# Scaling and splitting v on GpSimd, and one product in place of two for the remainder rows

## The chip, the cores and the metric

The kernel runs on one core of one Trainium2 chip. The metric is the device time of one execution in microseconds (us). The core has five engines that run side by side, each with a queue of its own that it works off in order: TensorE (PE in the profile, with its weight loads as PEld), VectorE (DVE), ScalarE (ACT), GpSimd (POOL) and SyncE (SP), which here issues all the transfers. Engines wait for one another through semaphores.

## The reference

Three parts follow one another, in fp32, for 4 batches of 576 rows and 512 columns (8 heads of 64).

1. Attention for each batch and head: `scores = q k^T / 8`; scores under the row's maximum less `tau` (0.02) are masked out; then softmax; the result is `attn @ v`. The heads are put side by side to 576 x 512.
2. A mixer: `u = x + (relu(x^T @ w_tok1) @ w_tok2)^T` (256 hidden tokens), then `u + relu(u @ w_ch1) @ w_ch2` (1536 hidden channels).
3. A gated part: `h = relu(x @ w_in)` (1024 channels), a convolution of 3 rows along the sequence with `conv_w`, `h * sigmoid(conv)`, and the product with `w_out`.

## The kernel before

**Numbers.** TensorE multiplies in f16, so each fp32 factor is split into a high half (its value rounded to f16) and a low half (the rest, rounded to f16), and a product is made of three: high x high, low x high and high x low. ScalarE writes the high half, VectorE or GpSimd the low one by subtraction. GpSimd works on SBUF only.

**Attention.** `attention(b)` goes over 36 slots for a batch: 4 pairs of heads with 9 slots each. A slot is a tile of 128 rows of one head, but slot 4 of a pair holds the last 64 rows of both heads, one head in each half of the partitions. These are the remainder rows. In each slot `scores` (line 300) multiplies on TensorE into PSUM; `exps` (321) takes the row maximum on VectorE (line 324), the threshold on ScalarE or, for batches 2 and 3, on GpSimd (line 332), and the exponentials on ScalarE (336); `mask` (340) masks on VectorE (343), `ph` (345) writes the high half on ScalarE (348) and `rest` (350) the low half on GpSimd (352), and behind it issues the transposing DMA (357). Five slots later `pv` (359) multiplies the transposed probabilities with v. A column of v that holds a constant gives the row sums.

**v.** `prep(b, p)` (229) prepares a pair of heads while the pair before it is worked on, in steps between the slots. It loads q, k and v, v into a tile of a pool `ld` with three buffers (line 268). For each of the two heads (loop of line 271) it then writes the high half `vh` of v times 16 on ScalarE (272), and the low half `vl` on VectorE (273), which scales and subtracts in one instruction over 128x320. That is 32 such halves of pairs in all. When the tile of v has been read for the last time it is free for a later load. `vh` and `vl` have two buffers.

**Norm.** `norm` (377) runs twice for a pair, when a head's last slot has been multiplied. On VectorE it takes the reciprocal of the row sums (383, 384) and multiplies it in (387). After the first head (`hh == 0`) it also does the remainder rows: a tiny instruction over 128x2 makes a factor `rm` for each half of the partitions from the constant `blk`, which holds ones and zeros (391), and a product with it spreads the rows to both heads' columns (392). ScalarE and GpSimd then split the result (397, 398).

**Dense part.** `tok` (400) does the first product pair of the mixer; `dense(b)` (507) the rest, with the gates (lines 574 to 588) between the products with `w_in` (598) and those with `w_out` (622). In the gates VectorE runs lines 583 and 586, whose inputs lie in SBUF, and GpSimd writes a low half (588). The dense part of batch b is interleaved with the attention of batch b + 1, so that TensorE always has some of both. The weights arrive and are split during the attention of batch 0 and the dense part of batch 0 (`wload`, 122).

**What sets the order.** The text calls the steps in an interleaved order, but a planner at build time sorts the instructions of each engine and of SyncE's queue anew, by when its own model of durations has them ready. In a few places (`issue_after`) the text holds an instruction behind another.

Of the kernel before, what the change touches and what calls it, by code (L numbers as in the profile page):

```python
# [8 lines left out]
F32 = mybir.dt.float32  # L9
# [3 lines left out]
AF = mybir.ActivationFunctionType  # L13
ALU = mybir.AluOpType
# [5 lines left out]
def kernel(ctx: ExitStack, tc: tile.TileContext, q, k, v, tau,  # L20
# [9 lines left out]
    H, D = 2 * NPR, 64  # L30
    P = 128
# [7 lines left out]
    NS = S // P  # L39
# [6 lines left out]
    VSC = 16.0  # L46
# [8 lines left out]
    const = ctx.enter_context(tc.tile_pool(name="const", bufs=1))  # L55
# [7 lines left out]
    sm = ctx.enter_context(tc.tile_pool(name="sm", bufs=6))  # L63
    psum = ctx.enter_context(tc.tile_pool(name="psum", bufs=1, space=PSUM))

    V, A, G, T = nc.vector, nc.scalar, nc.gpsimd, nc.tensor
# [8 lines left out]
    V.tensor_scalar_mul(ident, idf, 1.0 / UDS)  # L75
    ident2 = const.tile([P, 64], F16, name="ident2")
    V.tensor_tensor(out=ident2, in0=ident[:, 0:64], in1=ident[:, 64:P], op=ALU.add)
    blk = const.tile([P, 2], F32, name="blk")
    V.memset(blk, 0.0)
    V.memset(blk[0:64, 0:1], 1.0)  # L80
    V.memset(blk[64:P, 1:2], 1.0)
# [8 lines left out]
    for x, (sc, left) in enumerate(((0.125, 1.0), (QK, ESC))):  # L90
        V.tensor_scalar(out=qsc[:, x:x + 1], in0=tau_t, scalar1=0.0, scalar2=sc, op0=ALU.is_ge, op1=ALU.mult)
        V.scalar_tensor_tensor(out=mtaus[:, x:x + 1], in0=tau_t, scalar=-1.0 / left, in1=every,
                               op0=ALU.mult, op1=ALU.min)
# [14 lines left out]
    def hold(x):  # L108
        return tc.issue_after(turn[behind[x]].ins) if behind.get(x) in turn else nullcontext()
# [101 lines left out]
    def f32(t):  # L211
        return t.rearrange("p a s -> p (a s)").bitcast(F32)
# [12 lines left out]
    def split(out, t, sc):  # L225
        A.activation(out=out[:, 0], in_=t, func=AF.Copy, scale=sc)
        V.scalar_tensor_tensor(out=out[:, 1], in0=t, scalar=sc, in1=out[:, 0], op0=ALU.mult, op1=ALU.subtract)

    def prep(b, p):

        vh, vl = v_t[p % 2]
        qt, kt = qk_t[p % 2]
        pair[b, p] = dict(qt=qt, kt=kt, vh=vh, vl=vl)
        if b < NB32:
            with hold("qk") if b else nullcontext():
                nc.sync.dma_start(f32(qt), q[b, p])
                for h in range(2):
                    if b == 0 and p < 2:
                        G.memset(f32(kt[h])[(1 - h) * D:(2 - h) * D], 0.0)
                    nc.sync.dma_start(f32(kt[h])[h * D:(h + 1) * D], k[b, p, h * D:(h + 1) * D])  # L240
            if b:
                yield
                yield
            A.activation(out=f32(qt), in_=f32(qt), func=AF.Copy, scale=qsc[:, 0:1])
        else:
            qn, kn = [ld.tile([P, S], F32, tag="ld", name="ld") for _ in range(2)]
            with hold("qk"):
                nc.sync.dma_start(qn, q[b, p])
                nc.sync.dma_start(kn, k[b, p])
        if b >= NB32:  # L250
            yield
            qs = qk2.tile([P, 2, S], F16, tag="qs", name="qs")
            split(qs, qn, qsc[:, 1:2])
            for h in range(2):
                for x in range(2):
                    nc.sync.dma_start(qt[x * D:(x + 1) * D, h], qs[h * D:(h + 1) * D, x])
            yield
            ks = qk2.tile([P, 2, S], F16, tag="qs", name="ks")
            split(ks, kn, QK)
            for h in range(2):  # L260
                for r in range(2):
                    nc.sync.dma_start(kt[h][r * D:(r + 1) * D], ks[h * D:(h + 1) * D])
        yield
        vn = []
        for hh in range(2):
            t = ld.tile([P, S], F32, tag="ld", name="ld")
            with hold("qk") if b else nullcontext():
                nc.sync.dma_start(t, v[b, 2 * p + hh])
            vn.append(t.rearrange("p (a d) -> p a d", d=D))
        yield  # L270
        for hh in range(2):
            A.activation(out=vh[:, hh, :, 0:D], in_=vn[hh], func=AF.Copy, scale=VSC)
            V.scalar_tensor_tensor(out=vl[:, hh], in0=vn[hh][:, 0:NS + 1], scalar=VSC,
                                   in1=vh[:, hh, 0:NS + 1, 0:D], op0=ALU.mult, op1=ALU.subtract)
            yield

    def cut(slot):
# [81 lines left out]
    def pv(i):  # L359
        b, p, slot = where(i)  # L360
        st = pair[b, p]
        vh, vl, pt = st["vh"], st["vl"], chk.pop(i)["pt"]
        n = slot if slot <= NS else slot - NS - 1
        dst = ps[:, 7, n * (D + 1):(n + 1) * (D + 1)]
        for o, m, hh, _ in cut(slot):
            for j in range(NSL):
                T.matmul(dst[o:o + m], pt[:, j, o:o + m], vh[:, hh, j, 0:D + 1],  # L367
                         start=(j == 0), stop=(j == NSL - 1))
                if j <= NS:
                    T.matmul(dst[o:o + m, 0:D], pt[:, j, o:o + m], vl[:, hh, j], start=False, stop=False)  # L370
        if slot == 0:
            st["x32"] = p2.tile([P, NS + 1, P], F32, tag="x32", name="x32", bufs=1)
            st["xp"] = [p2.tile([P, NS + 1, P], F16, tag=f"x{x}", name=f"x{x}") for x in "hl"]
        if slot in (NS, NSL - 1):
            norm(ps[:, 7], st["x32"], st["xp"], 0 if slot == NS else 1)

    def norm(pvt, x32, xp, hh):


        n = NS + 1 - hh  # L380
        p3v = pvt[:, :n * (D + 1)].rearrange("p (a d) -> p a d", d=D + 1)
        rc = sm.tile([P, NS + 1, 1], F32, tag="rc", name="rc")
        V.tensor_scalar(out=rc[:, :n], in0=p3v[:, :, D:D + 1], scalar1=1e-9 * ONE, scalar2=None, op0=ALU.add)
        V.reciprocal(out=rc[:, :n], in_=rc[:, :n])
        cs = slice(hh * D, (hh + 1) * D)
        parts = [(slice(0, NS), cs)]
        V.tensor_tensor(out=x32[:, 0:NS, cs], in0=p3v[:, 0:NS, 0:D],  # L387
                        in1=rc[:, 0:NS].to_broadcast([P, NS, D]), op=ALU.mult)
        if hh == 0:
            rm = sm.tile([P, 2, 1], F32, tag="rm", name="rm")  # L390
            V.tensor_scalar(out=rm[:, :, 0], in0=blk, scalar1=rc[:, NS], scalar2=None, op0=ALU.mult)
            V.tensor_tensor(out=x32[:, NS].rearrange("p (h d) -> p h d", h=2),
                            in0=p3v[:, NS:NS + 1, 0:D].to_broadcast([P, 2, D]),
                            in1=rm.to_broadcast([P, 2, D]), op=ALU.mult)
            parts.append((slice(NS, NS + 1), slice(0, P)))
        for ss, cc in parts:
            A.activation(out=xp[0][:, ss, cc], in_=x32[:, ss, cc], func=AF.Copy)
            G.tensor_tensor(out=xp[1][:, ss, cc], in0=x32[:, ss, cc], in1=xp[0][:, ss, cc], op=ALU.subtract)
# [54 lines left out]
    def attention(b):  # L453
# [9 lines left out]
        for i in range(c0, c1, NSL):  # L463
            bb, p, _ = where(i + NSL)
            if bb < B:
                start(i - 1, prep(bb, p), (1, 2, 2, 1, 1, 1))
            start(i + NSL - 1 + LAG + 2, tok(b, where(i)[1]), (2, 1, 1))
        if b == 0:
            for _ in prep(0, 0):
                pass  # L470
# [242 lines left out]
```

## Time and profile before

| | |
|---|---|
| median of 3 runs | 825.0 us (823.21 to 829.17) |
| profiled execution | 827.29 us |
| its span, first to last instruction | 825.5 us |
| mean granted TensorE clock | 0.969 |
| TensorE busy | 757.0 us, 92% of the span |
| VectorE busy | 538.6 us, 65% |
| ScalarE busy | 496.4 us, 60% |
| GpSimd busy | 334.3 us, 40% |

The profile is of one execution. Busy time of an engine is that of its instructions; waits, branches and the issuing of DMAs don't count. An instruction that another engine holds up while it runs shows that as a longer duration. The chain of waits goes back from the last instruction, at each step to what released it, so it shows which work set the end. Times of single instructions are given in ns, all others in us.

### The profile page before, as it was taken

What the parts mean: (1) busy time and instruction counts of PE and PEld (TensorE: products, weight loads), DVE (VectorE), ACT (ScalarE), POOL (GpSimd) and SP (SyncE); (2) the same over time, 40 slices, a digit from 0 to 9 for tenths busy, and PEclk for the clock granted to TensorE, in tenths of its full rate; (3) what the DMA queues carried; (4) which work ended last, traced back from release to release, by engine and by line L of the source; (5) the groups of instructions that cost most, each with busy time, mean ns of one, the idle gap of its engine ahead of it and who ended that gap; (6) DMA issues with size and microseconds to landing.
All of it is one profiled execution on the core that took longest, in us unless ns stands there. A gap on an engine that the chain in (4) does not pass through costs nothing.

```text
span 825.5 us, 18489 instructions
## 1 busy us (share of the span) xinstructions
PE 757.0 (92%) x7376; PEld 566.8 (69%) x7376; DVE 538.6 (65%) x912; ACT 496.4 (60%) x1037; POOL 334.3 (40%) x338
## 2 busy tenths in 40 slices
PE   5588969989897968999999989999999999999988
PEld 3466757767676756577788766677888766777754
DVE  6888878887976799624277896166776970323370
ACT  7787878878876888634255786256655761221361
POOL 3566634335563577611034574034544640000040
PEclk9889989999998989999999999999999999999999
DMA  8999998789996866422047662237544411000001
GB/s 242 208 215 170 160 219 218 185 200 223 235 212 184 213 141 123 95 83 68 16 73 150 133 118 74 66 76 148 106 88 80 67 29 52 8 2 1 2 1 57
DMA packets 195046, 97.83 MB, mean 119 GB/s; under 512 B 174096, under 2 KB 176656, under 8 KB 194960
## 3 DMA queue, kind: packets, MB, share of 16 engines
q1 hardware_dynamic: 194960, 96.66, 53.9%
q8 instruction: 57, 0.93, 0.5%
q14 instruction: 29, 0.24, 0.1%
HBM read 42.36 MB, written 4.72 MB: 57 GB/s over the span
## 4 chain that ended last, share of the span: by engine, by line
PE 55%; DVE 17%; DMA 13%; ACT 8%; issue 4%; POOL 2%; SPq 0%; ACTq 0%; DVEq 0%; POOLq 0%
PE ps L565 13%; PE ps L547 12%; PE ps L622 9%; DMA pt<-ph 4%; DVE ct L583 4%; PE ps L598 4%; PE ps L308 3%; PE ps L312 3%; PE ps L367 3%; DVE nm L324 3%; DMA st<-in_moe_w_ch_dram 2%; DVE e L343 2%; PE ps L409 2%; PE ps L424 2%; PE ps L370 1%
## 5 line engine op out<-in xcount | busy, mean ns | idle before, releaser
L352 POOL TENSOR_TENSOR ph<-e,ph 128x576 f16<-128x576 f32 x108 | 145.0, 1346 | 145.2 <-ACT ph L348 134.4
L565 PE MATMUL ps<-act_t,wc_h 128*128 128x256 f16 (+1 forms) x768 | 151.4, 289 | 0.3 <-DVE us L529 0.2
L324 DVE TENSOR_REDUCE nm<-ps 128x1 f32<-128x576 f32 x144 | 107.7, 749 | 23.6 <-PE ps L312 16.4
L308 PE MATMUL ps<-kt,qt 128*128 128x288 f32 (+1 forms) x320 | 97.0, 454 | 27.1 <-DVE act_t L343 13.7
L343 DVE SCALAR_TENSOR_TENSOR e<-ps,thr,e 128x576 f32<-128x576 f32 x108 | 87.4, 812 | 41.1 <-ACT e L336 22.7
L547 PE MATMUL ps<-u_h,wc_h 128*128 128x320 f16 (+1 forms) x384 | 110.4, 288 | 1.4 <-DVE act_t L522 1.4
L565 PE MATMUL ps<-act_t,wc_l 128*128 128x256 f16 (+1 forms) x384 | 110.9, 289 | 0.0
L547 PE MATMUL ps<-u_h,wc_l 128*128 128x320 f16 (+1 forms) x384 | 110.3, 287 | 0.0
L547 PE MATMUL ps<-u_l,wc_h 128*128 128x320 f16 (+1 forms) x384 | 110.2, 287 | 0.0
L348 ACT ACTIVATE ph<-e 128x576 f16<-128x576 f32 x108 | 73.0, 679 | 42.6 <-DMA pt<-ph 21.5
L588 POOL TENSOR_TENSOR act_t<-ct,act_t 128x576 f16<-128x576 f32 x32 | 45.4, 1418 | 127.2 <-ACT act_t L587 124.2
L547 PEld LDWEIGHTS <-wc_h 128*128 128x128 f16 x768 | 75.3, 98 | 21.6 <-issue 1.5
L565 PEld LDWEIGHTS <-wc_h 128*128 128x128 f16 x768 | 75.8, 99 | 19.9 <-issue 0.5
L522 DVE SCALAR_TENSOR_TENSOR act_t<-ps,act_t 128x256 f16<-128x256 f32 (+1 forms) x96 | 43.4, 454 | 70.1 <-ACT act_t L521 69.9
L598 PE MATMUL ps<-u_h,wi_h 128*128 128x256 f16 (+1 forms) x256 | 73.8, 289 | 13.4 <-ACT h L574 7.4
L308 PEld LDWEIGHTS ps<-kt,qt 128*128 128x128 f32 (+1 forms) x320 | 52.9, 193 | 47.1 <-DVE act_t L343 19.0
L367 PE MATMUL ps<-vh,pt 128*128 128x65 f16 (+1 forms) x1080 | 74.1, 197 | 5.4 <-DVE x L387 2.7
L622 PE MATMUL ps<-wo_h,act_t 128*128 128x512 f16 x256 | 77.7, 383 | 0.4 <-POOL act_t L588 0.3
L583 DVE SCALAR_TENSOR_TENSOR ct<-h,cw,ct 128x576 f32<-128x576 f32 x64 | 71.9, 1124 | 7.6 <-ACT ct L581 6.9
L598 PE MATMUL ps<-u_l,wi_h 128*128 128x256 f16 (+1 forms) x256 | 74.0, 290 | 0.0
L598 PE MATMUL ps<-u_h,wi_l 128*128 128x256 f16 (+1 forms) x256 | 73.9, 289 | 0.0
L367 PEld LDWEIGHTS <-pt 128*128 128x128 f16 (+1 forms) x1080 | 63.9, 102 | 14.6 <-issue 6.5
(119 smaller groups left out, 1606.1 us busy)
## 6 DMA issues: line engine op xcount, KB each, us to landing
st<-in_moe_w_ch_dram SPq DMA_DIRECT2D x24, 512.0 KB, 4.2
ld<-in_v_dram SPq DMA_DIRECT2D x32, 288.0 KB, 3.9
kt<-ks SPq DMA_DIRECT2D x32, 144.0 KB, 2.7
st<-in_moe_w_in_dram SPq DMA_DIRECT2D x8, 512.0 KB, 3.7
st<-in_moe_w_out_dram SPq DMA_DIRECT2D x8, 512.0 KB, 4.4
out_dram<-ot SPq DMA_DIRECT2D x16, 256.0 KB, 2.0
qt<-in_q_dram SPq DMA_DIRECT2D x8, 288.0 KB, 4.4
kt<-in_k_dram SPq DMA_DIRECT2D x16, 144.0 KB, 4.3
```

The lines of the kernel that those rows point to most:

```text
L308: T.matmul(s3[o:o + m, a], f32(st["qt"])[:, q0:q0 + m], f32(st["kt"][hh])[:, a * hn:(a + 1) * hn], start=True, stop=True)
L324: crit["max"] = V.tensor_reduce(out=nm, in_=c["s3"], axis=AX.XY, op=ALU.max, negate=True)
L343: crit["mask"] = V.scalar_tensor_tensor(out=e3, in0=c["s3"], scalar=c["thr"], in1=e3, op0=ALU.is_ge, op1=ALU.mult)
L348: A.activation(out=c["ph"][:, 0:S], in_=c["e"], func=AF.Copy)
L352: G.tensor_tensor(out=c["ph"][:, S:], in0=c["e"], in1=c["ph"][:, 0:S], op=ALU.subtract)
L367: T.matmul(dst[o:o + m], pt[:, j, o:o + m], vh[:, hh, j, 0:D + 1], start=(j == 0), stop=(j == NSL - 1))
L547: T.matmul(t, wc1[wx][:, f, c], u[c][ux][:, sl], start=(c == 0 and i == 0), stop=(c == NC - 1 and i == 2))
L565: T.matmul(t, wc2[wx][:, c, f], r_t(f, rx)[:, sl], start=(by_dve(c) and f == 0 and i == 0), stop=(f == NF - 1 and i == 2))
L583: V.scalar_tensor_tensor(out=ct, in0=ht[:, kk:kk + S], scalar=cw[:, kk, f:f + 1], in1=ct, op0=ALU.mult, op1=ALU.add)
L588: G.tensor_tensor(out=g_t(f, 1), in0=ct, in1=g_t(f, 0), op=ALU.subtract)
L598: T.matmul(t, wi[wx][:, f, c], u[c][ux][:, s0:s0 + n], start=(c == 0 and i == 0), stop=(c == NC - 1 and i == 2))
L622: T.matmul(t, g_t(f, gx)[:, j * P:(j + 1) * P], wo[wx][:, f], **lim)
```

## The change

v is scaled by 16 on GpSimd, in place, in its load tile. ScalarE's copy then takes the scaled tile, without a scale of its own, and GpSimd subtracts to give the low half, where VectorE scaled and subtracted before. In `norm` the factor `rm` is no longer made: one instruction multiplies the remainder rows in PSUM with the reciprocal, as a scalar of each partition, and with `blk`, as the second operand.

```diff
-    blk = const.tile([P, 2], F32, name="blk")
+    blk = const.tile([P, 2, 1], F32, name="blk")
...
         for hh in range(2):
-            A.activation(out=vh[:, hh, :, 0:D], in_=vn[hh], func=AF.Copy, scale=VSC)
-            V.scalar_tensor_tensor(out=vl[:, hh], in0=vn[hh][:, 0:NS + 1], scalar=VSC,
-                                   in1=vh[:, hh, 0:NS + 1, 0:D], op0=ALU.mult, op1=ALU.subtract)
+            G.tensor_scalar(out=vn[hh], in0=vn[hh], scalar1=VSC, scalar2=1.0, op0=ALU.mult, op1=ALU.mult)
+            A.activation(out=vh[:, hh, :, 0:D], in_=vn[hh], func=AF.Copy)
+            G.tensor_tensor(out=vl[:, hh], in0=vn[hh][:, 0:NS + 1], in1=vh[:, hh, 0:NS + 1, 0:D], op=ALU.subtract)
             yield
...
         if hh == 0:
-            rm = sm.tile([P, 2, 1], F32, tag="rm", name="rm")
-            V.tensor_scalar(out=rm[:, :, 0], in0=blk, scalar1=rc[:, NS], scalar2=None, op0=ALU.mult)
-            V.tensor_tensor(out=x32[:, NS].rearrange("p (h d) -> p h d", h=2),
-                            in0=p3v[:, NS:NS + 1, 0:D].to_broadcast([P, 2, D]),
-                            in1=rm.to_broadcast([P, 2, D]), op=ALU.mult)
+            V.scalar_tensor_tensor(out=x32[:, NS].rearrange("p (h d) -> p h d", h=2),
+                                   in0=p3v[:, NS:NS + 1, 0:D].to_broadcast([P, 2, D]), scalar=rc[:, NS],
+                                   in1=blk.to_broadcast([P, 2, D]), op0=ALU.mult, op1=ALU.mult)
             parts.append((slice(NS, NS + 1), slice(0, P)))
```

## Rows read from the trace of the kernel before

**Rows 1.** The page: busy time of the engines; shares of the chain of waits.

```profile
PE 757.0 (92%) x7376; PEld 566.8 (69%) x7376; DVE 538.6 (65%) x912; ACT 496.4 (60%) x1037; POOL 334.3 (40%) x338
...
PE 55%; DVE 17%; DMA 13%; ACT 8%; issue 4%; POOL 2%; SPq 0%; ACTq 0%; DVEq 0%; POOLq 0%
```

**Rows 2.** Windows: stretch, length, busy us (instructions) PE, PEld, DVE, ACT, POOL; clock, DMA.

```profile
14.00:105.00 91.00, 72.34 (x797) 53.92 (x798) 79.61 (x131) 74.14 (x160) 56.01 (x50) 0.91 1.00 192
105.00:370.00 265.00, 236.58 (x2266) 174.65 (x2264) 203.85 (x346) 197.66 (x407) 133.25 (x124) 0.94 0.77 180
370.00:460.00 90.00, 90.00 (x927) 72.36 (x926) 49.76 (x94) 39.74 (x88) 23.58 (x31) 1.00 0.41 84
460.00:505.00 45.00, 41.26 (x459) 31.20 (x457) 40.47 (x54) 34.73 (x72) 30.30 (x27) 1.00 0.55 109
```

**Rows 3.** The chain of waits by line, from 14 to 106 us.

```profile
by line: PE ps L308 13.7%; DMA act_t<-act_t 13.0%; DVE act_t L343 10.5%; DVE nm L324 10.3%; issue 7.0%; PE ps L367 5.7%; DVE wf L157 4.6%; DVE vl L273 4.3%; DMA qt<-in_q_dram 3.6%; DVE rm L391 3.2%; PE ps L370 2.7%; ACT act_t L348 2.6%; ACT
```

**Rows 4.** Pieces of the chain of waits: start us, us on it, what.

```profile
139.77 0.94 DVE rm L391
...
270.50 1.18 DVE vl L273
...
271.70 4.66 DMA ld<-in_k_dram
...
664.71 0.40 DVE rm L391
```

**Rows 5.** Groups by line: line engine operation out<-in xcount | busy us, mean ns | idle before.

```profile
L273 DVE SCALAR_TENSOR_TENSOR vl<-ld,vh 128x320 f16<-128x320 f32 x32 | 20.5, 641 | 4.7 <-ACT vh L272 4.6
...
L391 DVE TENSOR_SCALAR rm<-blk,rc 128x2 f32<-128x2 f32 x16 | 9.5, 596 | 0.0
```

**Rows 6.** Single lines on VectorE and ScalarE: xcount, ns min/median/max, first and last start us.

```profile
L273 DVE SCALAR_TENSOR_TENSOR vl<-ld,vh x32: 452/482/1456, 8.3 to 608.2; 128x320 f16<-128x320 f32 x32
...
L391 DVE TENSOR_SCALAR rm<-blk,rc x16: 213/504/1154, 38.7 to 664.6; 128x2 f32<-128x2 f32 x16
...
L392 DVE TENSOR_TENSOR x<-ps,rm x16: 274/276/293, 41.2 to 665.7; 128x128 f32<-128x128 f32 x16
...
L272 ACT ACTIVATE vh<-ld x32: 666/682/691, 7.6 to 606.6; 128x576 f16<-128x576 f32 x32
```

**Rows 7.** The same view, lines on GpSimd.

```profile
L352 POOL TENSOR_TENSOR ph<-e,ph x108: 1271/1280/1898, 104.8 to 662.0; 128x576 f16<-128x576 f32 x108
...
L146 POOL TENSOR_TENSOR wt_l<-wf,wt_h x4: 728/822/1175, 30.7 to 47.7; 128x288 f16<-128x288 f32 x4
...
L239 POOL MEMSET kt<- x4: 571/572/578, 1.0 to 3.1; 64x576 f32 x4
```

**Rows 8.** Waits: who <- for whom: us in total, times, longest us.

```profile
POOL ph L352 <- ACT ph L348: 134.4, 74, 6.9
...
ACT ph L348 <- DMA pt<-ph: 21.5, 18, 3.2
...
DVE e L343 <- POOL thr L332: 17.7, 14, 3.0
```

**Rows 9.** Waits of SyncE's queue, in the same form.

```profile
SPq L268 <- DVE vl L273: 13.1, 4, 8.5
```

**Rows 10.** Timeline of VectorE: start us, us, line, operation.

```profile
66.24 0.86 DVE L391 TENSOR_SCALAR rm<-blk,rc 128x2 f32<-128x2 f32 x1
67.01 0.74 DVE L324 TENSOR_REDUCE nm<-ps 128x1 f32<-128x576 f32 x1
```

**Rows 11.** Windows of line 273 alone: stretch, length, busy us (instructions), clock, DMA.

```profile
0.00:345.00 345.00, 15.28 (x22) 0.93 0.87 193
285.00:345.00 60.00, 3.01 (x3) 0.91 0.63 131
450.00:510.00 60.00, 2.33 (x4) 1.00 0.55 115
```

**Rows 12.** A line of the gates on VectorE: xcount, ns min/median/max, starts.

```profile
L583 DVE SCALAR_TENSOR_TENSOR ct<-h,cw,ct x64: 801/819/1947, 288.1 to 803.7; 128x576 f32<-128x576 f32 x64
```

## The prediction

> **What bounds the kernel now.** I read the page's busy times and the engine shares of its chain of waits first [rows 1]. TensorE is busy 92% and holds 55% of the chain; VectorE is busy 538.6 us and holds 17% of the chain, some 140 us; GpSimd is busy 334.3 us and holds 2%, some 16 us. So an average us on VectorE lands on the chain with a chance of about 26% (140 / 538.6), one on GpSimd with about 5% (16.5 / 334.3). That makes a move from VectorE to GpSimd look cheap, but shares are means over unlike stages, so the table by stretch comes next [rows 2]. From 370 to 460 us TensorE is busy in all of 90.00 us: nothing taken off VectorE can be gained there. From 14 to 105 us, the attention of batch 0, it is busy 72 of 91 us and VectorE 79.6, which is 87%. From 460 to 505 us, where the gates run, VectorE is busy 40.5 of 45 us and GpSimd 30.3.
>
> The chain of waits by line for 14 to 106 us [rows 3] gives line 273 4.3% and line 391 3.2%, together 7.5% of 92 us or 6.9 us. After 106 us there are ten more pieces of the two lines on the chain, from 139.77 to 664.71 us (the first, two others and the last in [rows 4]), with a sum of 6.0 us. Both edits together therefore touch 12.9 us of the chain. That is the bound on what can be gained directly.
>
> **The change, part by part.** *The low halves of v leave VectorE.* 32 instructions of line 273 take 20.5 us, 641 ns each in the mean, though the shortest took 452 and the longest 1456 [rows 5, 6]. Nothing inside the instruction explains a factor of three; it reads two tiles in SBUF, and it is longest where GpSimd is also busy. *The remainder factor.* 16 tiny instructions of line 391 (128x2) take 9.5 us, 596 ns each, from 213 to 1154 [rows 5, 6], and they go. What replaces lines 391 and 392 is one instruction over the same 128x128 elements with its first operand in PSUM and only the constant in SBUF. Its price is that of line 392, 276 ns; its lower end is the 274 of the same row, and its upper end is line 391's longest added, 1154 + 276, if it met the same obstacle. I take 0.28, because lines 392 and 273 differ in just that: the one with a PSUM operand spans 274 to 293 ns, the one with two SBUF inputs 452 to 1456. VectorE loses 20.5 + 9.5 = 30.0 us of its 538.6.
>
> *GpSimd gains 64 instructions.* The subtraction over 128x320 lies between two rows of the same kind [rows 7]: 728 ns for 288 elements and 1271 for 576 at their shortest, so 1.89 ns an element and 0.79 us. The scaling over 128x576 has one input, and no row shows such an instruction at this width. A memset of 576 elements took 573 ns, which only writes; the two-input subtraction of 576 took 1271. With one input read as fast as it is written it lies nearer the memset: I take 0.70 us and keep 0.57 and 1.27. So GpSimd gets 32 x (0.70 + 0.79) = 47.7 us, and goes from 334 to 382 us (between 378 and 400 with collisions left out). At its 5% of chain per busy us that costs 2.3 us.
>
> *The order of waits.* Before, ScalarE waited for the load of v and VectorE for ScalarE. Now GpSimd waits for the load, ScalarE's line 272 for GpSimd, and GpSimd again for ScalarE. Queued behind GpSimd's wait are line 352's low halves of the probabilities, which release the transposing DMAs, and line 332's thresholds, which line 343 on VectorE already awaited for 17.7 us in 14 places [rows 8]. ScalarE's copy keeps its length, since line 348 does the same without a scale. One release moves too: SyncE's queue waited 13.1 us in four places for line 273 before it could load v again [rows 9], and on the chain a piece of line 273 at 270.50 us is followed at once by a load of k of 4.66 us [rows 4]. That release now comes at the end of GpSimd's subtraction, 0.34 us later by length alone (0.79 - 0.45), plus its place in GpSimd's queue. The DMAs issued are the same in number and size.
>
> **The sum.** In 14 to 106 us VectorE is near its limit, but transposes and TensorE's scores are next in line: on the chain there, PE L308 and DMA act_t have 13.7% and 13.0% [rows 3]. I count two thirds of the 6.9 us, 4.6. Of the ten later pieces, seven with 4.5 us lie before 370 us, where the weights arrive and TensorE is busy 89% [rows 2]: half, 2.2 us. The last three, 1.5 us, lie later, two of them in the stretch from 460 us, where TensorE is busy 92%: a third, 0.5 us. Gain 7.3, cost on GpSimd 2.3, net 5.0 us. The profiled execution took 827.3 us (825.5 of span and 1.8 around it), which becomes 822.3. It lies 2.3 us above the median of the runs shown, 825.0, so against that median I forecast **820.0 us**. The two thirds, half and third are choices; with all or nothing in their place the forecast would be 814 or 827. The price of the two extra handovers has no row: below, the 4.7 us that VectorE stood before line 273 [rows 5] may go; above, it is rival B.
>
> **A thing that no row settles** is the order on each engine. It isn't the text's: line 392 follows line 391 in the code, but VectorE ran line 324 behind line 391 [rows 10]. A planner sorts by its own durations, so other durations on two engines can shift places far from the edit. I put 3 us on either side for that.
>
> **The rivals.** *A, everything shows.* The 12.9 us all vanish, and VectorE, with 30 us less, finishes its gates sooner. GpSimd hides its 47.7 us in its idle time, of which 134.4 us were waits for line 348 alone [rows 8]. 825.0 - 12.9 = 812, and to 808 with some of the other collisions gone. Against it: TensorE and the DMAs are next in line nearly everywhere.
>
> *B, slower: GpSimd's queue becomes the late server.* The mechanism: GpSimd starts the subtraction only after ScalarE's copy (0.68 us [rows 6], and its place in that queue), and stands meanwhile, so each half holds line 352 back by 1.49 + 0.7 = 2.2 us. The transposes behind it come late, and ScalarE's line 348, which already waited 21.5 us in 18 places for a transpose to free its buffer [rows 8], stands longer. It decides where GpSimd has no slack: 22 of the 32 halves lie before 345 us [rows 11], outside TensorE's full stretch. If 45% of 2.2 us shows on each, that is 22 us, less the 12.9 us taken off: 834; if 60% shows, 29 us and 841. For it: GpSimd is at 62% from 14 to 105 us and would go to 75%. Against it: its 2% of the chain.
>
> *C, nothing is left over: 825, 821 to 829.* GpSimd's new work collides with VectorE's gates instead. Line 583 reads two tiles in SBUF and takes 801 ns at its shortest and 1947 at its longest [rows 12]. Seven halves lie in the first two gate stretches (285 to 345 and 450 to 510 us [rows 11]), so 14 new GpSimd instructions, each able to hold one such instruction back by up to 1.1 us and by half that in the mean, 8 us if all meet one. That and the cost on GpSimd eat the 7.3 us. The Trainium skill, SBUF — State Buffer, section "Who interferes with whom", has a rule for this: a VectorE instruction with two SBUF inputs contends with a GpSimd instruction that reads SBUF, and one with at most one SBUF input outside the two-port modes does not. Lines 391, 273 and 583 bear it out in their spread. By that rule the new remainder product is safe, and lines 583 and 586 are not. The same skill's GPSIMD Engine Reference, section "Engine selection", advises against elementwise work with two inputs on GpSimd, as about 2 times slower. No run here shows both for the same tile; the rows give 452 ns on VectorE and my estimate of 790 on GpSimd, 1.7 times.
>
> *That the change doesn't do what it says* can hardly be: both edits replace instructions one by one.
>
> **The chances.** Forecast (816 to 824 and its edges) 0.44, A 0.16, B 0.18, C 0.22. A measurement here tells no change from about 1%, 816.8 to 833.3 us. Faster than that: A nearly whole and a quarter of the forecast, 0.26, and a little for a luckier order, 0.28. Slower: most of B, 0.16, with an unlucky order 0.18. The rest is 0.54 within 1%. Range 809 to 834: it leaves out the far ends of A and of B.
>
> **What would show it.** VectorE's busy time near 508 us and GpSimd's near 382; the new remainder product at 0.28 us each time; GpSimd's subtraction at 0.79; the span from 14 to 106 us shorter by some 5 us. Wrong it is if line 352 shows longer waits behind the new GpSimd lines and ScalarE's line 348 waits much longer than 21.5 us for transposes (B), if line 583 takes longer in the mean (C), or if the scaling costs over 1.27 us.

## The result, and the profile after

The changed kernel takes 818.5 us in the median of 9 runs (815.0 to 821.3), against 825.8 us in 9 runs of the kernel before (820.7 to 829.2). The ratio is 0.9911, with a 95% interval from 0.9882 to 0.9939: 7.3 us or 0.9% faster, where 820.0 was forecast. Below, ratios to the kernel before are turned into us at 825 us; each comes from runs on the same chip.

The page after: busy times.

```profile
PE 745.4 (91%) x7376; PEld 560.3 (69%) x7376; DVE 520.4 (64%) x864; ACT 497.0 (61%) x1037; POOL 384.2 (47%) x402
```

Against [rows 1], GpSimd has 49.9 us more, about as many as forecast (47.7). VectorE has 18.2 us less, not 30.0. The page's chain of waits can't be set beside the one of before: its shares add up to about a third of the span, and from 14 to 105 us it has no piece.

The same stretches as in [rows 2], after: stretch, length, busy us (instructions) on PE, PEld, DVE, ACT, POOL, then clock and DMA.

```profile
14.00:105.00 91.00, 72.46 (x846) 53.36 (x846) 74.18 (x125) 77.17 (x167) 69.49 (x68) 0.94 0.96 196
105.00:370.00 265.00, 234.22 (x2251) 174.34 (x2252) 195.73 (x325) 194.72 (x402) 148.32 (x143) 0.97 0.76 176
370.00:460.00 90.00, 90.00 (x987) 73.71 (x986) 54.98 (x97) 46.75 (x100) 36.23 (x47) 1.00 0.53 103
460.00:505.00 45.00, 39.61 (x431) 28.75 (x429) 37.26 (x47) 31.89 (x66) 33.31 (x29) 1.00 0.45 97
```

From 14 to 105 us VectorE's load fell from 79.6 to 74.2 us and GpSimd's rose from 56.0 to 69.5, to 76% of the stretch.

The new lines, with ns min/median/max and first and last start: 272 scales on GpSimd, 273 copies on ScalarE, 274 subtracts on GpSimd, 390 is the remainder product.

```profile
L272 POOL TENSOR_SCALAR ld<-ld x32: 670/670/1069, 7.7 to 560.2; 128x576 f32<-128x576 f32 x32
...
L273 ACT ACTIVATE vh<-ld x32: 666/678/713, 8.4 to 598.1; 128x576 f16<-128x576 f32 x32
...
L274 POOL TENSOR_TENSOR vl<-ld,vh x32: 755/771/1286, 9.2 to 598.9; 128x320 f16<-128x320 f32 x32
...
L390 DVE SCALAR_TENSOR_TENSOR x<-ps,rc,blk x16: 337/341/343, 38.2 to 655.7; 128x128 f32<-128x128 f32 x16
```

The product runs at 337 to 343 ns in all 16 places, where line 391 spread from 213 to 1154 [rows 6]. In the trace of before, each of the twelve places where line 391 took 247 ns or more ends 24 to 28 ns behind the end of a GpSimd instruction. One is the first line of [rows 10], which ends at 67.10 us; GpSimd beside it:

```profile
65.79 1.28 POOL L352 TENSOR_TENSOR act_t<-act_t 128x576 f16<-128x576 f32 x1 [2.13 <-ACT act_t L348]
```

The new product has a GpSimd instruction beside it in 14 of its 16 places and is not held up. The rule that the forecast cited (Trainium skill, SBUF — State Buffer, "Who interferes with whom") says so of an instruction with at most one SBUF input outside the two-port modes, and the trace agrees. Line 391 too read one tile in SBUF besides its scalar, so the number of inputs alone doesn't tell the two apart; no run here shows in which mode it ran.

Where much of the other 12 us of VectorE's relief went is seen in its groups by line (busy us, mean ns, then idle before). Before:

```profile
L583 DVE SCALAR_TENSOR_TENSOR ct<-h,cw,ct 128x576 f32<-128x576 f32 x64 | 71.9, 1124 | 7.6 <-ACT ct L581 6.9
...
L227 DVE SCALAR_TENSOR_TENSOR qs<-ld,qsc,qs 128x576 f16<-128x576 f32 x8 | 7.2, 905 | 3.1 <-ACT qs L226 2.7 <-DMA kt<-ks 0.3
```

After (line 581 is line 583 of before):

```profile
L581 DVE SCALAR_TENSOR_TENSOR ct<-h,cw,ct 128x576 f32<-128x576 f32 x64 | 75.8, 1184 | 11.2 <-ACT ct L579 10.4
...
L227 DVE SCALAR_TENSOR_TENSOR qs<-ld,qsc,qs 128x576 f16<-128x576 f32 x8 | 8.4, 1054 | 4.6 <-ACT qs L226 4.6
```

The gates' line costs 3.9 us more and the split of q 1.2 more, though neither was touched: both read two tiles in SBUF while GpSimd is busier. All untouched lines together cost 7.3 us more, and the new product 1.0 more than line 392. The rest, 3.5 us, is in the counting: the durations of neighbours on VectorE overlap in the records (the first line of [rows 10] ends at 67.10 us, the next starts at 67.01), so they add up to 584.2 us before where the busy time is 538.6. A sum of durations overstates what the engine is relieved of.

Waits after, for [rows 8]: us in total, times, longest us.

```profile
POOL ph L352 <- ACT ph L348: 98.0, 59, 4.4
...
POOL ld L272 <- DMA ld<-in_v_dram: 22.4, 14, 4.5
...
POOL vl L274 <- ACT vh L273: 20.9, 17, 3.9
...
DVE e L343 <- POOL thr L332: 18.1, 17, 2.3
...
ACT ph L348 <- DMA pt<-ph: 11.7, 10, 2.7
```

GpSimd now stands 43.3 us for the load of v and for ScalarE's copy, and line 352's waits fell by 36. The wait of line 348 for transposes fell from 21.5 to 11.7 us: GpSimd's queue did not become the late server of rival B.

**Where the time came from.** Two milestones tell it: the first start of the products with `w_in` and of the stores of the result, first in the profile before (the two numbers after the durations are first and last start).

```profile
L598 PE MATMUL ps<-u_h,wi_h x256: 269/296/474, 276.9 to 797.5; 128*128 128x256 f16 x64, 128*128 128x320 f16 x64
...
L609 SPq DMA_DIRECT2D out_dram<-ot x16: 332/338/530, 352.3 to 819.5; - x16
```

And after:

```profile
L596 PE MATMUL ps<-u_h,wi_h x256: 269/296/472, 265.3 to 788.3; 128*128 128x256 f16 x64, 128*128 128x320 f16 x64
...
L607 SPq DMA_DIRECT2D out_dram<-ot x16: 332/338/579, 341.4 to 810.3; - x16
```

Batch 0's dense part reaches `w_in` 11.6 us earlier and its first store 10.9 us earlier; the last store is 9.1 us earlier. So the gain is there by some 345 us. But the 11.6 us are not all time won. The order moved these products past scores of the next batch (line 308 multiplies the scores of batches 0 and 1), first before, then after:

```profile
L308 PE MATMUL ps<-kt,qt x320: 406/406/850, 6.2 to 255.7; 128*128 128x288 f32 x128, 128*64 128x288 f32 x32
...
L308 PE MATMUL ps<-kt,qt x320: 405/407/850, 6.1 to 270.7; 128*128 128x288 f32 x128, 128*64 128x288 f32 x32
```

Before, the last of them starts ahead of the first `w_in` product, after it 5 us behind. And little of the gain lies in the attention of batch 0, where the forecast saw most: line 348 on ScalarE starts with the first slot of batch 1 at 101.3 us after 103.9, a gain of 2.6 us.

### The profile page after: what moved, and what is told of

The parts are those of the page before. It is cut to its first block, busy times and chain, and to the rows that moved or that the text cites. A ratio compares the mean times of both kernels' runs of the same rounds, so it can differ in the third digit from the quotient of the medians.

```text
span 816.2 us, 18497 instructions
## 1 busy us (share of the span) xinstructions
PE 745.4 (91%) x7376; PEld 560.3 (69%) x7376; DVE 520.4 (64%) x864; ACT 497.0 (61%) x1037; POOL 384.2 (47%) x402
## 5 line engine op out<-in xcount | busy, mean ns | idle before, releaser
L352 POOL TENSOR_TENSOR ph<-e,ph 128x576 f16<-128x576 f32 x108 | 142.7, 1323 | 105.3 <-ACT ph L348 98.0
L563 PE MATMUL ps<-act_t,wc_h 128*128 128x256 f16 (+1 forms) x768 | 148.9, 286 | 0.3 <-DVE rl L413 0.3
L308 PE MATMUL ps<-kt,qt 128*128 128x288 f32 (+1 forms) x320 | 92.8, 448 | 18.5 <-DVE act_t L343 8.8
L586 POOL TENSOR_TENSOR act_t<-ct,act_t 128x576 f16<-128x576 f32 x32 | 49.8, 1555 | 123.6 <-ACT act_t L585 120.5
L596 PE MATMUL ps<-u_h,wi_h 128*128 128x256 f16 (+1 forms) x256 | 74.2, 290 | 11.7 <-ACT h L572 7.1
L581 DVE SCALAR_TENSOR_TENSOR ct<-h,cw,ct 128x576 f32<-128x576 f32 x64 | 75.8, 1184 | 11.2 <-ACT ct L579 10.4
L596 PE MATMUL ps<-u_l,wi_h 128*128 128x256 f16 (+1 forms) x256 | 74.2, 291 | 0.0
```

Of the source, the lines that this page charges most:

```text
L308: T.matmul(s3[o:o + m, a], f32(st["qt"])[:, q0:q0 + m], f32(st["kt"][hh])[:, a * hn:(a + 1) * hn], start=True, stop=True)
L352: G.tensor_tensor(out=c["ph"][:, S:], in0=c["e"], in1=c["ph"][:, 0:S], op=ALU.subtract)
L563: T.matmul(t, wc2[wx][:, c, f], r_t(f, rx)[:, sl], start=(by_dve(c) and f == 0 and i == 0), stop=(f == NF - 1 and i == 2))
L581: V.scalar_tensor_tensor(out=ct, in0=ht[:, kk:kk + S], scalar=cw[:, kk, f:f + 1], in1=ct, op0=ALU.mult, op1=ALU.add)
L586: G.tensor_tensor(out=g_t(f, 1), in0=ct, in1=g_t(f, 0), op=ALU.subtract)
L596: T.matmul(t, wi[wx][:, f, c], u[c][ux][:, s0:s0 + n], start=(c == 0 and i == 0), stop=(c == NC - 1 and i == 2))
```

## The experiments

Theory 1, the prediction's: VectorE's relief itself gives the time. Theory 2: the planner's new order gives it. Theory 3, named in two expectations: TensorE's granted clock gives it. The two programs share 7216 instructions on TensorE (7376 records in the trace), and 3368 of them have another place in its queue; on ScalarE it is 552 of 1036, on SyncE 146 of 353.

### One edit alone

The remainder product alone (the diff's last part, with `blk`):

> Only the remainder product is changed; v is scaled and split as before. Theory 1 (VectorE relief): lines 391 and 392 held 4.9 of the 12.9 us that both edits touch on the chain, and VectorE loses some 8 us of busy time, so 40% of the whole gain of 7 us: 822 to 823 us. Theory 2 (order): the planner's new order, and not the work taken off, set the gain; then this kernel lies anywhere from 818 to 831 us, without regard to its 8 us. Theory 3 (clock): TensorE's time at the lower granted clock falls with the time, from 51 us in the profile before.

Measured: 822.7 us, ratio 0.9987 (0.9961 to 1.0013), -1.1 us.

v alone (the diff's middle part):

> Only v's scaling and low halves go to GpSimd; the remainder rows keep their two instructions. Theory 1: VectorE loses 20.5 us, 8.0 us of it on the chain, GpSimd gets 50 us; 60% of the gain: 820 to 822 us. Together with the norm-only kernel the two gains add up to that of the change, 7 us. Theory 2: they don't add up; either may lie on either side of 825. Theory 3: the time follows TensorE's time at the lower clock.

Measured: 821.1 us, 0.9970 (0.9950 to 0.9990), -2.5 us. Each falls within theory 1's numbers, but the two make 3.6 us (plus or minus 2.7) and not 7.3 (2.4). That they don't add up speaks for theory 2, though only just beyond the noise. One pair of runs speaks against theory 3: the profiled run of v alone had a clock of 0.983, as that of the change, and took 823.4 us against 818.0.

### Without the scaling

```diff
-    VSC = 16.0
-    ONE = 0.125
+    VSC = 1.0
+    ONE = 0.125 / 16
...
-            G.tensor_scalar(out=vn[hh], in0=vn[hh], scalar1=VSC, scalar2=1.0, op0=ALU.mult, op1=ALU.mult)
```

> The change without its scaling instruction: v is split as it is loaded, and the constant column is 16 times smaller in its place, so the result keeps its scale. GpSimd loses 32 x 0.67 = 21 us of busy time and one handover for each half of a pair. If GpSimd's load costs what the prediction said, 5% of its busy time, it gains 1 us on the change: 817 to 818. If GpSimd's queue is a late server (rival B partly true), it gains 5 us or more: 813 or less. If order rules, 812 to 825.

Measured: 818.5 us, 0.9922 (0.9896 to 0.9949), the time of the change. GpSimd is busy 24.5 us less than in the change (359.7), and nothing measurable comes of it; the planner ordered this kernel anew too. It beats the kernel before, but not the changed one.

### A harmless instruction on either side

In the kernel before, and below in the changed one:

```diff
+    scr = const.tile([P, 1], F32, name="scr")
...
+            G.tensor_scalar(out=scr, in0=vn[hh][:, 0, 0:1], scalar1=VSC, scalar2=1.0, op0=ALU.mult, op1=ALU.mult)
```

> A control: the kernel before with one tiny GpSimd instruction more for each half of a pair (128x1, from v's load tile to a scrap tile, some 0.26 us, 8 us in all). It takes nothing off VectorE. Theory 1: 825 to 827 us. Theory 2: the planner's order changes here as well, so the time moves by several us to one side or the other. Whatever it moves by is the size of the order's effect.

Measured: 827.0 us, 1.0022 (1.0001 to 1.0042), +1.8 us, which both theories allow.

> The control on the other side: the changed kernel with a GpSimd instruction of 128x1 more for each half of a pair, from v's load tile to a scrap tile. The same addition to the kernel before cost 2 us. Theory 1: 818 to 821 us, since VectorE keeps its relief. Theory 2 (a lucky order): the luck goes with the order, and the time goes back to 821 to 825.

Measured: 824.4 us, 1.0008 (0.9983 to 1.0033). That is 8.1 us (plus or minus 3.1) over the change, for 32 instructions that take this on GpSimd:

```profile
L273 POOL TENSOR_SCALAR scr<-ld x32: 191/192/714, 8.0 to 568.3; 128x1 f32<-128x1 f32 x32
```

They are 7.5 us of busy time (235 ns in the mean) on an engine that is idle half of the time, and nobody waits for what they write. The whole gain of the change goes with them. Theory 2 had said so. This control was not repeated with the order held, so what the instructions cost by themselves is not separated.

### Load on one engine alone

VectorE's load put back into the changed kernel:

```diff
+    scr = const.tile([P, NS + 1, D], F32, name="scr")
...
+            V.scalar_tensor_tensor(out=scr, in0=vh[:, hh, 0:NS + 1, 0:D], scalar=1.0, in1=vl[:, hh], op0=ALU.mult, op1=ALU.subtract)
```

> The changed kernel with one VectorE instruction more for each half of a pair: 128x320 with two inputs in SBUF (vh and vl), into a scrap tile, so VectorE has its 32 subtractions again while nothing waits for them and GpSimd keeps its new work. Theory 1 (VectorE relief): VectorE's some 20 us come back and with them the gain of moving v: 822 to 826 us. If the relief is not the cause (theory 2, order, or that what counted was the place of the low halves in the chain): 816 to 820.

Measured: 825.9 us, 1.0023 (1.0007 to 1.0038). The added line with its spread:

```profile
L276 DVE SCALAR_TENSOR_TENSOR scr<-vh,vl x32: 448/866/1567, 10.0 to 611.6; 128x320 f32<-128x320 f16 x32
```

By itself this is what theory 1 asks for. But after the control it proves nothing, since the planner's order changed here as well. It does show the collision once more: 448 ns at its shortest, 866 in the median, with GpSimd busy 387 us beside it.

GpSimd's load put into the kernel before:

```diff
+    scr = const.tile([P, 2 * NS + 1, D], F16, name="scr")
...
+            G.tensor_scalar(out=scr, in0=vn[hh], scalar1=VSC, scalar2=1.0, op0=ALU.mult, op1=ALU.mult)
             A.activation(out=vh[:, hh, :, 0:D], in_=vn[hh], func=AF.Copy, scale=VSC)
...
+            G.tensor_tensor(out=scr[:, 0:NS + 1], in0=scr[:, 0:NS + 1], in1=vh[:, hh, 0:NS + 1, 0:D], op=ALU.subtract)
```

> The kernel before with GpSimd's new work added and nothing taken off VectorE: a scaling over 128x576 from v's load tile and a subtraction over 128x320 with vh, both into a scrap tile (f16), so GpSimd waits for the load and for ScalarE as in the change, but nobody waits for its results. By the prediction's price, 5% of some 47 us: 2 to 3 us over the before, 827. Rival B: 835 or more. A collision cost (rival C) of 4 us and more on VectorE's two-input instructions: 828 to 832.

Measured: 819.7 us, 0.9949 (0.9928 to 0.9970): 4.2 us faster with 53 us more to do on GpSimd and nothing taken off. No theory of load can explain that sign.

The tiny instruction put back into the changed kernel:

```diff
+            rm = sm.tile([P, 2, 1], F32, tag="rm", name="rm")
+            V.tensor_scalar(out=rm[:, :, 0], in0=blk[:, :, 0], scalar1=rc[:, NS], scalar2=None, op0=ALU.mult)
```

> The changed kernel with the tiny instruction that made the factor (128x2) put back, its result unused. Theory 1: it took 9.5 us on VectorE and 4.9 us of the chain; the move of v alone gave 821.1, so this lands at 820 to 822. If the two edits only help together through the planner's order, anything from 816 to 826.

Measured: 830.4 us, 1.0086 (1.0062 to 1.0110), 14.5 us over the change by the ratios, for 16 instructions of 9.4 us in all. Outside theory 1's numbers, and outside what I allowed theory 2.

### The same work in the other's order

Four kernels keep the planner but fix its order: behind the last traced instruction, an edge goes from each instruction of an engine to the one that stood ahead of it in the other kernel's program. The edges order the issue and add no wait. `ORDER` holds the positions.

```diff
+    for eng, steps_ in json.loads(zlib.decompress(base64.b85decode("".join(ORDER)))).items():
+        mine = [x for x in nc.cur_bb.bb.instructions if str(x.engine) == "EngineType." + eng
+                and type(x).__name__ not in ("BassTilePoolBoundary", "InstRegisterMove")
+                and (eng == "Activation" or x.debug.lineno not in free_lines)]
+        row = [mine[n + d] for n, d in enumerate(steps_)]
+        for x, y in zip(row, row[1:]):
+            tc.add_manual_dep(y, x.name, mybir.DependencyInfo(mybir.DependencyClass.NoSync, mybir.DependencyReason.DATA),
+                              reason="order")
```

The instructions on `free_lines`, those that only one of the kernels has, stay with the planner. The traces show that the hold works: read line by line, without the edited lines, the old and the new order differ in 2124 of TensorE's 7376 places and on every other engine too, while each of the four has the order that it was given, in every place on every engine. No kernel was held in its own order, so what the edges do to the time by themselves is not measured.

> The changed kernel's instructions, held in the order of the kernel before: on TensorE, ScalarE, VectorE, GpSimd and SyncE's queue every instruction that both kernels have stands where the planner of the kernel before put it, by edges that fix the issue order and add no wait. Only GpSimd's 64 new instructions find their place freely. Theory 1 (the work itself): VectorE's 30 us are gone as in the change, so 818 to 820 us. Theory 2 (the order): the gain came with the new order, so 822 to 826. If half and half: 821.

Measured: 828.2 us, 1.0058 (1.0034 to 1.0081). The changed work in the old order is 4.8 us slower than the kernel before. Its page and milestones:

```profile
PE 745.7 (90%) x7376; PEld 558.0 (68%) x7376; DVE 516.9 (63%) x864; ACT 495.2 (60%) x1037; POOL 383.2 (46%) x402
```

```profile
L596 PE MATMUL ps<-u_h,wi_h x256: 269/290/300, 277.8 to 798.1; 128*128 128x256 f16 x64, 128*128 128x320 f16 x64
...
L607 SPq DMA_DIRECT2D out_dram<-ot x16: 332/338/532, 352.4 to 820.1; - x16
```

VectorE has its relief (516.9 us), yet `w_in` starts at 277.8 and the first store at 352.4 us: the times of the kernel before.

> The other corner: the instructions of the kernel before, held in the changed kernel's order; only the 48 instructions of lines 273 and 391 find their place freely. Theory 1: 824 to 826 us. Theory 2: 817 to 820. Half and half: 821. The two corners with the kernel before and the changed one make a square, and the effects of work and order are its two sides.

Measured: 819.8 us, 0.9964 (0.9939 to 0.9988), -3.0 us. Its page and milestones:

```profile
PE 744.8 (91%) x7376; PEld 560.4 (69%) x7376; DVE 539.6 (66%) x912; ACT 498.2 (61%) x1037; POOL 340.9 (42%) x338
```

```profile
L598 PE MATMUL ps<-u_h,wi_h x256: 269/296/417, 266.7 to 789.4; 128*128 128x256 f16 x64, 128*128 128x320 f16 x64
...
L609 SPq DMA_DIRECT2D out_dram<-ot x16: 332/340/572, 343.2 to 811.4; - x16
```

VectorE is as loaded as before (539.6 us), and `w_in` starts at 266.7 us and the store at 343.2: the times of the changed kernel, within 2 us. The milestones go with the order and not with the work. A part of the order's effect can be placed: from 300 to 345 us, in the gates of batch 0. The stretch in the kernel before, the changed one, new work in the old order, old work in the new order (stretch, length, busy us on PE, PEld, DVE, ACT, POOL, clock, DMA):

```profile
300.00:345.00 45.00, 39.71 (x378) 27.47 (x377) 39.68 (x56) 34.72 (x71) 32.63 (x29) 0.92 0.54 106
...
300.00:345.00 45.00, 42.70 (x390) 27.81 (x389) 32.48 (x44) 32.06 (x66) 34.93 (x33) 0.99 0.52 112
...
300.00:345.00 45.00, 36.50 (x369) 25.56 (x367) 36.89 (x52) 33.16 (x70) 36.60 (x33) 1.00 0.53 106
...
300.00:345.00 45.00, 41.47 (x387) 27.60 (x386) 34.73 (x48) 33.07 (x67) 34.55 (x31) 1.00 0.57 111
```

The last three have the clock at 0.99 or 1.00, so their busy times can be compared: TensorE is busy 42.7 and 41.5 us in the new order, with either work, and 36.5 in the old order with the new work. The square, as ratios to the kernel before:

| | order of before | order of the change |
|---|---|---|
| work of before | 1 | 0.9964 |
| work of the change | 1.0058 | 0.9911 |

The order is worth -3.0 us (plus or minus 2.0) with the old work and -12.1 us (3.0) with the new. The work is worth +4.8 us (1.9) in the old order and -4.4 us (3.1) in the new. Means over the square: order -7.6, work +0.2 us. But the order's two prices differ by 9.1 us (3.7), and so do the work's, so neither has a price of its own: the work pays in the order that was planned for it, and costs in the one that was not.

> The changed kernel with the tiny 128x2 instruction put back, its result unused, this time in the changed kernel's order; left to the planner it took 830.4 us, 12 us over the change. Theory 1: the instruction itself, held up by GpSimd for a mean of 0.6 us, cost the 12 us, and it does so again: 828 to 831. Theory 2: the planner's order cost them, so with the order held it is 819 to 822, its 9.5 us of VectorE's time showing in part.

Measured: 821.8 us, 0.9991 (0.9967 to 1.0016). (The expectation's 12 us compare medians of different chips; by the ratios it is 14.5.) With the order held, the tiny instruction costs 6.7 us (3.1) over the change, and the other 7.8 us (2.8) that it cost without were the planner's. Its row there:

```profile
L391 DVE TENSOR_SCALAR rm<-blk,rc x16: 217/524/1159, 38.9 to 657.1; 128x2 f32<-128x2 f32 x16
```

It is the row of before again, with its collisions. So leaving out this one instruction is worth about 7 us in the new order, where line 391 held 4.9 us of the chain. It runs ahead of the remainder product, which frees a bank of PSUM that TensorE's line 367 needs: that line waited 5.7 us for it here and 3.1 in the changed kernel. The rest of the 6.7 us was not traced.

In the last kernel, lines 273 and 391 are free beside the added ones:

> The kernel before with GpSimd's load of the change added, its results unused, in the order of the kernel before; left to the planner it took 819.7 us, 4.7 us less than the before although it has more to do. Theory 2 says that this was the order's gift, so with the order held the load shows its true price: the prediction's 2 to 3 us (827), or more if GpSimd's queue is a late server (rival B, 830 and over). If the added work itself had helped (by holding something back at a good place), 819 to 822.

Measured: 825.9 us, 1.0036 (1.0014 to 1.0057), +3.0 us. The gift of 4.2 us is gone and the load shows a price, its collisions with VectorE included (busy 544.3 us against 538.6). The added lines there:

```profile
L273 POOL TENSOR_SCALAR scr<-ld x32: 672/673/1212, 7.8 to 593.5; 128x576 f16<-128x576 f32 x32
...
L277 POOL TENSOR_TENSOR scr<-scr,vh x32: 738/754/1252, 8.6 to 605.4; 128x320 f16<-128x320 f16 x32
```

## Why the prediction was right, and where only its number was

The time, the sign and the range were right. The sum behind them holds only in part.

- **Prices.** The scaling at 0.70 us took 0.67 at its shortest and 0.70 in the mean (22.4 us for 32), the subtraction at 0.79 took 0.77 in the median and 0.86 in the mean; GpSimd's busy time came to 384 us against 382. Taking the scaling to be nearer a memset than a two-input subtraction was right. The remainder product took 341 ns and not 276: line 392, a product of two operands, was the wrong row for one with a scalar beside them. That is 1 us over 16.
- **VectorE's relief**, 30 us, came to 18. Of the missing part 7.3 us went into untouched lines, most of it into those that read two tiles in SBUF (581: +3.9 us). That is rival C's mechanism. The forecast gave it to a rival, but left it out of its own busy time of 508 us. Another 3.5 us were never there: the 30.0 is a sum of durations that overlap.
- **The cost of GpSimd's load**, 2.3 us by its share of the chain, was 3.0 us (1.2 to 4.7) with the order held. The term agrees with that, and rival B had the wrong size.
- **The step that does not hold** outside the order that came out is "Gain 7.3": pieces of the chain times a share that shows. In the order of the kernel before, the new work loses 4.8 us, of which 3.0 is GpSimd's load; so relief and handovers together come to a loss of 1.8 us (2.6), and not to a gain of 7.3. A piece on the chain is what ended last in one order of work. Taken away, it leaves the rest of that order standing: there, the first `w_in` product came no earlier at all. In the new order the sum fares better: the work is worth -4.4 us (3.1) there, where the forecast's net was -5.0.
- **The second is the size given to the order**, "3 us on either side". The square has 3.0 and 12.1 us; two kernels with and without a held order differ by 7 and 8 us, and the control in the changed kernel cost 8. The order was named as the thing that no row settles, and was priced as a tail where it was as large as the rest. That the forecast of -5.0 met -7.3 is then partly luck: work and order came out together, and each depends on the other.
- **From 14 to 106 us**, 4.6 us of gain was forecast and 2.6 came; in the corner with new work and old order the same start lies at 102.8 us, 1.1 us of gain, with VectorE at 73.6 of 91 us. Unloading VectorE, busy 87% there, did not shorten the stretch by much.
- **TensorE's clock** moved with the time. Over the runs the mean granted clock is 0.985 in the changed kernel, 0.976 in the new work with the old order and 0.983 in the old work with the new order, against 0.975 and 0.976 in two sets of the kernel before. Within the kernels, 0.01 more of it goes with 2.3 us less (234 runs), so up to some 2 us of the 7.3 may come with it. The clock does not carry the order's effect: the profiled runs of the new work in the new and in the old order both have 0.983, with TensorE busy 745.4 and 745.7 us, and took 818.0 and 827.9 us. Whether its small part is a cause or follows from fuller queues was not separated.

What stays open is which of the moved instructions carry the order's effect. The milestones place it between 105 and 345 us, and with the new work TensorE's busy time puts some 6 us of the 12 between 300 and 345. Holding one engine's order at a time would tell; it wasn't tried.

## What to carry to other kernels

Where a planner sorts the queues, an edit is two changes: the work, and a new order everywhere. Before a gain under 1% is put down to the work, run a control that adds something harmless, and hold the order fixed in a corner or two: here they showed an order worth 3 us with the old work and 12 with the new, behind a change of 7. And a relief counted in pieces of the chain of waits is a bound for the order that gave the chain, not a forecast.

## What the runs showed of the hardware that was not expected

- A VectorE instruction that multiplies a PSUM operand with a scalar of each partition and with an SBUF operand took 341 ns over 128x128, where the product of a PSUM and an SBUF operand took 276 [rows 6]: 65 ns more. The two-operation form by itself does not show that: with a constant as its scalar (line 415 of before) it took 418 ns over 128x256, the plain product (line 387) 415. So the scalar read per partition is the likely cause; it was not tested alone.
- A GpSimd scaling of 128x576 took 670 ns with f32 written and 672 with f16 written, and one of 128x1 took 191, so by an estimate from these two sizes about 0.83 ns an element beside a fixed 0.19 us. The two-input form has 1.89 ns an element between the rows of 288 and 576 [rows 7], though its 320 took 755 ns at the shortest and not the 788 that this gives.
- A VectorE instruction over 128x2, 213 ns at its shortest, waits out the GpSimd instruction that is running: it took up to 1154 ns and ended 24 to 28 ns behind that one. The wait shows as a longer duration and not as idle time (line 391: idle 0.0 [rows 5]). In the new order 16 of them cost the kernel 6.7 us (plus or minus 3.1).
